# The first group's second product as seven products in seven PSUM banks, and the second group's attention between the units of its first product

## Chip, cores and metric

One core of a Trainium2 chip runs the kernel. The metric is the device time of one execution, in microseconds; lower is better.

## What is computed

The first part is a lightning attention over `q`, `k`, `v` of shape (4, 8, 768, 64) in float32: in blocks of positions, scores are masked by powers of a decay `lam`, and a state `k^T v` is carried from block to block. The second part takes its result as a matrix `x` of 3072 tokens by 512 and runs two products with an activation between them:

```python
x = attn_out.transpose(0, 2, 1, 3).reshape(3072, 512)
h = x @ w_in                  # 512 x 2048
g = h - np.tanh(h)
out = g @ w_out               # 2048 x 512, float32
```

The two weight matrices arrive as 64-bit floats. The kernel makes 32-bit floats of them itself.

## The kernel before

**Tiling.** The tokens are worked in six groups (`NG`), group g holding block g of 128 positions of all four batches, so 512 tokens. The 2048 hidden columns are four units (`NU`) of 512. Each group has attention for two pairs of batches (`attention(g)`: transposes, scores, output, state), the first product `x @ w_in` unit by unit, the activation, and the second product with `w_out`.

**Seven products in place of eight.** Groups 1 to 5 do both matrix products by the Winograd scheme: each factor is cut in four, sums of the parts are formed, and seven products of half size take the place of eight (`FACT` lists which sums meet in which product). Some of those products are cut once more (`down_twice`, `inner_steps`). Group 0 does neither, because its weights are still arriving: `up_plain(u, (c,))` makes one quarter c of unit u (11, 21, 12 or 22) by eight calls of a 128x128 by 128x256 matmul, then a tanh on ScalarE (L760) and a subtraction on VectorE (L761) put it into `hidden(0, c)`. `down_plain(kt)` (L766) then makes the second product row block by row block: for each of eight row blocks `kt` it issues eight matmuls 128x128 by 128x512 (L774), two for each of four batches, into four PSUM banks that stay open over all eight row blocks. Float32 matmuls are two instructions each in the trace, a pair of weight load and matmul for each of two passes.

**How weights arrive.** `load_weights` starts the DMA of a 128x512 block of 64-bit weights into one of four `raw64` buffers: blocks 0 to 15 are `w_in` (four for each unit, on SP's queue), blocks 16 to 31 are `w_out` (two for each row block, on POOL's queue). `weights(n)` makes the blocks up to n ready by `round_block`: three operations on ScalarE (L269 to L271) and two on VectorE (L273, L274), through one of two scratch tiles `r0`, `r1`. A block's buffer is free again after its last ScalarE operation. Calls of `weights` stand by hand between the units and the row blocks, and so set how far the loads run ahead.

**Row blocks and their stores.** A row block `kt` of `w_out` lies in one of two buffers `wt` (pool `wst`), which has room for four parts and four sums. `sums_out(kt)` (L244) forms the sums on VectorE (L247 to L250) and stores seven factors to DRAM on POOL's queue: two DMAs into `factors` (L252, L253) and one or two into `fine` (L256). The later groups read them from there. The next row block to use a buffer waits until its matmuls, sums and stores have ended. `sums_in(u)` (L237) forms in place, on VectorE, the sums of `w_in` that the groups from 1 on need.

**Order.** After group 0's attention the body runs `up_plain` for units 0 to 3 (L817 to L825), then the eight row blocks (L829 to L837). The pieces of group 1's attention stand behind row blocks 0 to 5 (`more`, L828), and `sums_in` behind the last four. Then the pools `stage`, `qpool` and `wst` close, `load_quarters` fetches factors back, and the loop over groups 1 to 5 begins with `up(1, 0, 1)` (L847). A scheduler may move instructions of one engine a little against this order where `keep_in_program_order` (or `tied`) doesn't forbid it; each engine executes its own list strictly in order.

Of the kernel before, what the change touches and what calls it, by code (L numbers as in the profile page):

```python
# [9 lines left out]
F32 = mybir.dt.float32  # L10
# [5 lines left out]
AF = mybir.ActivationFunctionType  # L16
AL = mybir.AluOpType

BLK = 128
# [5 lines left out]
def kernel(  # L25
# [32 lines left out]
    nc = tc.nc  # L58
    B, H, S, D = q.shape
    NTOK, DM = out.shape  # L60
    DFF = moe_w_in.shape[1]
    NP = H // 2
    KI = DM // 128
# [3 lines left out]
    NU = DFF // 512  # L67
    KH = KO // 2
# [35 lines left out]
    def powers():  # L104
        for j in range(2):
            tc.keep_in_program_order(nc.vector.tensor_copy(
                fwd[ts(j, 64), :, 0], lam_all.rearrange("s (p j) -> s j p", j=2)[ts(j, 64), j, :]))
        m = 1
        while m < BLK:
            tc.keep_in_program_order(nc.vector.tensor_tensor(  # L110
                fwd[:, :, m:2 * m], fwd[:, :, 0:m], fwd[:, :, m - 1:m].to_broadcast([128, NP, m]), op=AL.mult))
            m *= 2
# [68 lines left out]
    NX = 7  # L181
    factors = dram.tile([NX, 128, KH, 256], F32, name="factors")

    SUB = (1, 2, 6, 5, 7, 3, 4)
# [37 lines left out]
    def weights(n):  # L222

        while ready["done"] < min(n, len(blocks)):
            at_ = ready["done"]
            load_weights(at_ + WAHEAD)
            kind, n_, m = blocks[at_]
            if kind == "out" and m == 0:
                pair[n_] = wst.tile([128, 8, 256], F32, name="wt", tag="w")
            w = w1[n_][:, m] if kind == "in" else pair[n_][:, 2 * m:2 * m + 2]  # L230
            if at_ in wraw:
                round_block(w, wraw.pop(at_), at_ < 2 * KI)
            else:
                load_block(nc.gpsimd, w, kind, n_, m)
            ready["done"] += 1

    def sums_in(u):  # L237
        a11, a12, a21, a22 = (w1[u][:, 2 * c:2 * c + 2, r] for r, c in ((0, 0), (0, 1), (1, 0), (1, 1)))
# [3 lines left out]
            tc.keep_in_program_order(nc.vector.tensor_tensor(dst, x, y, op=op))  # L242

    def sums_out(kt):  # L244
        wt = pair[kt]
        b11, b12, b21, b22, t1, t2, t4, t3 = (wt[:, x] for x in range(8))
        nc.vector.tensor_tensor(t1, b12, b11, op=AL.subtract)  # L247
        nc.vector.tensor_tensor(t2, b22, t1, op=AL.subtract)
        nc.vector.tensor_tensor(t3, b22, b12, op=AL.subtract)
        nc.vector.tensor_tensor(t4, b21, t2, op=AL.subtract)  # L250
        f = factors[:].rearrange("x p k c -> p x k c")
        nc.gpsimd.dma_start(out=f[:, 0:1, kt, :], in_=wt[:, 0:1, :])  # L252
        nc.gpsimd.dma_start(out=f[:, 1:NX, kt, :], in_=wt[:, 2:8, :])  # L253

        for x, j in ((1, 0),) if kt % 2 == 0 else ((2, 0), (3, 1)):
            nc.gpsimd.dma_start(out=fine[:, SUB.index(x), :, kt // 2, :].rearrange("n p c -> p n c"),  # L256
                                in_=wt[:, 3:8, ts(j, 128)])

    def round_block(w, raw64, first):

# [15 lines left out]
    def bank(name, tag, bufs):  # L276
        return psum.tile([128, 512], F32, name=name, tag=tag, bufs=bufs)
# [143 lines left out]
    def hidden(g, c):  # L421

        if (g, c) not in hid:
            hid[g, c] = gpool.tile([128, NU, 2, HB], F32, name=f"g{c}", tag=f"g{c}")
        return hid[g, c]
# [198 lines left out]
    def otile(name):  # L624
        return opool.tile([128, 512], F32, name=name, tag="o")
# [99 lines left out]
    def every(steps):  # L725
        for _ in steps:
            pass
# [15 lines left out]
    def up_plain(u, cs):  # L743

        hm = {}
        for c in cs:
            a, t = divmod(c - 11, 10)
            hm[c] = bank("h", ("ya", "yb", "z", "w")[2 * t + a], 1).rearrange("q (m c) -> q m c", m=2)
        for i in range(KI):
            for c in cs:  # L750
                a, t = divmod(c - 11, 10)
                for m in range(2):
                    tied(u == 0, nc.tensor.matmul(  # L753
                        out=hm[c][:, m, :], lhsT=w1[u][:, i, a, ts(m, 128)], rhs=xt[0, t][:, i, :],
                        start=m == 0 and i == 0, stop=i == KI - 1, skip_group_check=True))
                if (i, c) != (KI - 1, cs[-1]):
                    yield
        for c in cs:
            th = work.tile([128, 2, HB], F32, name="th", tag="th")
            nc.scalar.activation(th, hm[c], AF.Tanh)  # L760
            nc.vector.tensor_tensor(hidden(0, c)[:, u], hm[c], th, op=AL.subtract)  # L761
        yield

    obank = {}

    def down_plain(kt):  # L766
        wt = pair[kt]
        for b in range(B):
            if kt == 0:
                obank[b] = bank("op0", ("ya", "yb", "z", "w")[b], 1)  # L770
            i, t = divmod(b, 2)
            for a in range(2):
                g = hidden(0, 11 + i + 10 * a)[:, kt // 2, kt % 2, ts(t, 128)]
                nc.tensor.matmul(out=obank[b], lhsT=g, rhs=wt[:, 2 * a:2 * a + 2, :], start=kt == 0 and a == 0,  # L774
                                 stop=kt == KH - 1 and a == 1)
            if kt == KH - 1:
                ob = opool.tile([128, DM], F32, name="ob", tag="o")
                nc.scalar.activation(ob, obank[b], AF.Copy)
                nc.gpsimd.dma_start(out=out[b * S:b * S + BLK, :], in_=ob)


    def run(pieces):
        for fn, *args in pieces:
            fn(*args)
# [30 lines left out]
    every(half)  # L815
    weights(2 * KI)
    every(up_plain(0, (12, 22)))  # L817
    for u in range(1, NU):
        for c in (11, 21, 12, 22):
            every(up_plain(u, (c,)))  # L820
            weights(ready["done"] + 1)
        if u == 2:
            load(2 * B)
        if u == 1:
            powers()  # L825
    p0, p1 = attention(1)
    weights(len(blocks) - 2 * (KH - 2))
    more = [p0[0:1], p0[1:2], p0[2:], p1[0:1], p1[1:2], p1[2:]]  # L828
    for kt in range(KH):  # L829
        down_plain(kt)  # L830
        sums_out(kt)
        if kt + 2 < KH:
            weights(ready["done"] + 2)
        if kt < len(more):
            run(more[kt])
        if kt >= KH - NU:
            sums_in(kt - KH + NU)  # L837
    early.close()
    late["blk"] = ctx.enter_context(tc.tile_pool(name="blk", bufs=2 * B - 1))
    late["pool"] = ctx.enter_context(tc.tile_pool(name="late", bufs=1))  # L840
# [7 lines left out]
    for g in range(1, NG):  # L848
        last = g == NG - 1
        p0, p1 = attention(g + 1) if not last else ([], [])  # L850
        for u in range(NU):
            for n in (2, 6, 5, 7, 1, 4, 3) if g < GI else (1, 7, 3) if u == 0 else (6, 5, 1, 7, 3) if u + 1 < NU else (
                    6, 5, 7, 1, 3):
                if n != 1:
                    up(g, u, n)
                elif u + 1 < NU:
                    up(g, u + 1, 1)
                else:
                    every(down(g, 1))
                if g in turns:  # L860
                    made.append(n)
                    step = len(made) - turns[g][0]
                    for t, first in turns[g][1]:
                        if step == first:
                            if t > 1:
                                load_quarters(t)
                            making[t] = factors_twice(t)
                        if first <= step < first + 4:
                            next(making[t])
            if g == GI - 1:  # L870
                inner_weights(u)
            if not last and u > 1:
                run(p0[u - 2:u - 1])
        if twice(g, 4):
            sums_twice(g, 4)
        every(down(g, 2))
        run(p0[2:])
        sums_twice(g, 5)
        every(down_twice(g, 4, "z") if twice(g, 4) else down(g, 4))
        run(p1[0:1])  # L880
        sums_once(g, 21, 21, 11)
        sums_twice(g, 6)
        every(down_twice(g, 5, "w"))
        run(p1[1:2])
        if twice(g, 7):
            sums_twice(g, 7)
        every(down_twice(g, 6, "z"))
        if twice(g, 3):
            sums_twice(g, 3)
        run(p1[2:])  # L890
        every(down_twice(g, 7, "w") if twice(g, 7) else down(g, 7))
        if last:
            down_end(g)
            continue
        inner_tokens(g + 1)
        p3 = down_twice(g, 3, "z") if twice(g, 3) else down(g, 3)
        p2 = inner_steps(g + 1, 2, "yb")
        for kind, _ in in_turn(g):
            next(p3 if kind == "down" else p2)
        every(p2)  # L900
        every(p3)
        p4 = inner_steps(g + 1, 4, "yb")
        for n in (None, None, 1, None, None, 6, None, None, 5, None):
            if n is None:
                next(p4)
            else:
                up(g + 1, 0, n)
        every(p4)
# [30 lines left out]
```

## Time and profile before

| | us |
|---|---|
| median of 3 runs | 675.35 (675.31 to 678.8) |
| the profiled execution: its own time | 675.67 |
| its span in the profile | 673.8 |
| TensorE (PE) busy in the span | 661.6 |
| VectorE (DVE) busy | 451.1 |
| ScalarE (ACT) busy | 214.8 |
| GpSimd (POOL) busy | 199.5 |

The page gives, for each engine, busy time and its share of the span, then slices, DMA queues, the chain of work that ended last, and groups of instructions by line. 1.87 us of the profiled execution's time lie outside its span. A line number with L is one of the kernel before, unless it is said to be the changed kernel's.

### The profile page before, as it was taken

To read this page: it belongs to the slowest core of one execution; us is meant where nothing else is said; L and a number is where in the kernel's file an instruction comes from. 1 tells how busy PE (TensorE), PEld (TensorE's weight loads), DVE (VectorE), ACT (ScalarE), POOL (GpSimd) and SP (SyncE) were. 2 spreads that over 40 slices of the span, in tenths; PEclk is the share of its full clock that TensorE was granted. 3 is DMA by queue.
4 is the path that set the end of the run, shared out by engine and by line. 5 is a ranking of instruction groups with operands and counts; after the bars stand their busy time and mean duration, and the time that the engine had idled before them with its cause. 6 is when DMAs were issued, how large, how long until landed. Compare 5 with 4: busy or idle time off the path is not lost.

```text
span 673.8 us, 12802 instructions
## 1 busy us (share of the span) xinstructions
PE 661.6 (98%) x4824; PEld 576.0 (85%) x4824; DVE 451.1 (67%) x808; ACT 214.8 (32%) x405; POOL 199.5 (30%) x345
## 2 busy tenths in 40 slices
PE   8899999999999999999999999999999999999997
PEld 6688855458888999988999988899988899988997
DVE  4476454792887772499896378888358977357743
ACT  4797454523321111333112243112333122234110
POOL 0002333235332334144345201254300245400351
PEclk9999999999999999999999999999999999999999
DMA  9979769788655978587798742698830677610494
GB/s 210 220 223 288 258 202 286 231 242 244 178 142 129 242 200 212 123 249 230 219 287 254 186 79 51 157 280 245 245 75 8 164 235 217 217 38 1 126 293 160
DMA packets 162716, 128.79 MB, mean 191 GB/s; under 512 B 133856, under 2 KB 135008, under 8 KB 162656
## 3 DMA queue, kind: packets, MB, share of 16 engines
q0 software_dynamic: 28976, 96.49, 45.2%
q1 hardware_dynamic: 133536, 31.50, 23.7%
q8 instruction: 38, 0.62, 0.4%
q14 instruction: 22, 0.18, 0.1%
q10 hardware_dynamic: 144, 0.00, 0.0%
HBM read 103.55 MB, written 24.38 MB: 190 GB/s over the span
## 4 chain that ended last, share of the span: by engine, by line
PE 92%; DMA 2%; SPq 2%; issue 1%; POOL 1%; ACT 0%; DVE 0%; POOLq 0%; ACTq 0%
PE y L436 16%; PE z L436 10%; PE y L698 10%; PE op L774 8%; PE h L753 7%; PE zw L698 7%; PE w L645 5%; PE y L645 5%; PE y L520 4%; PE plain L645 3%; PE sp L330 3%; PE op L384 3%; PE z L520 2%; PE op L378 2%; PE kv L352 1%
## 5 line engine op out<-in xcount | busy, mean ns | idle before, releaser
L610 POOL DMA_DIRECT2D wb<-fine x147 | 79.2, 539 | 115.0 <-PE y L698 48.3
L444 ACT ACTIVATE th<-g 128x512 f32<-128x512 f32 x76 | 47.6, 630 | 99.0 <-DVE g L449 33.2
L613 POOL DMA_DIRECT2D wb<-factors x56 | 30.2, 541 | 155.6 <-PE y L645 97.3
L436 PE MATMUL y<-xt,w 128*128 128x256 f32 x320 | 74.0, 380 | 0.0
L436 PEld LDWEIGHTS y<-xt,w 128*128 128x128 f32 x320 | 59.9, 190 | 9.0 <-ACT g L524 0.9
L701 ACT ACTIVATE q<-y 128x128 f32<-128x128 f32 x84 | 23.3, 278 | 129.2 <-PE y L698 124.4
L445 DVE TENSOR_TENSOR g<-g,th 128x512 f32<-128x512 f32 x76 | 52.0, 690 | 18.2 <-ACT th L444 18.1
L753 PE MATMUL h<-xt,w 128*128 128x256 f32 x256 | 56.5, 381 | 1.3 <-DVE w L274 1.3
L774 PE MATMUL op<-wt,g 128*128 128x512 f32 x128 | 56.5, 595 | 0.0
L753 PEld LDWEIGHTS h<-xt,w 128*128 128x128 f32 x256 | 48.2, 190 | 8.5 <-DVE w L274 1.0
L698 PE MATMUL y<-wb,g 128*128 128x128 f32 x384 | 51.1, 278 | 0.0
L774 PEld LDWEIGHTS op<-wt,g 128*128 128x128 f32 x128 | 23.8, 190 | 27.7 <-issue 26.5
L698 PEld LDWEIGHTS y<-wb,g 128*128 128x128 f32 x384 | 46.4, 192 | 1.2 <-issue 0.3
L436 PE MATMUL z<-tt,ws 128*128 128x256 f32 x160 | 38.0, 380 | 0.0
L436 PE MATMUL z<-xt,ws 128*128 128x256 f32 x160 | 37.9, 380 | 0.0
L436 PE MATMUL y<-tt,ws 128*128 128x256 f32 x160 | 37.8, 379 | 0.0
L645 PE MATMUL y<-wb,g 128*128 128x256 f32 x160 | 35.6, 379 | 0.5 <-PE y L436 0.5
L645 PE MATMUL w<-wb,g 128*128 128x256 f32 x160 | 35.8, 382 | 0.0
L334 DVE TENSOR_TENSOR ss<-sp,mask 128x512 f32<-128x512 f32 x48 | 31.1, 685 | 6.3 <-PE sp L330 6.3
L645 PEld LDWEIGHTS y<-wb,g 128*128 128x128 f32 x160 | 30.3, 190 | 5.0 <-PE y L436 0.9
L205 POOL DMA_DIRECT2D raw<-in_moe_w_out_dram x16 | 9.3, 583 | 83.8 <-DMA raw<-in_moe_w_in_dram 52.0
L436 PEld LDWEIGHTS z<-xt,ws 128*128 128x128 f32 x160 | 30.3, 190 | 4.3 <-ACT g L452 0.2
(168 smaller groups left out, 1293.2 us busy)
## 6 DMA issues: line engine op xcount, KB each, us to landing
wb<-fine POOLq DMA_DIRECT2D x147, 256.0 KB, 4.1
wb<-factors POOLq DMA_DIRECT2D x68, 256.0 KB, 4.2
raw<-in_moe_w_out_dram POOLq DMA_DIRECT2D x16, 512.0 KB, 6.6
v_nat<-in_v_dram SPq DMA_DIRECT2D x24, 256.0 KB, 5.4
factors<-wt POOLq DMA_DIRECT2D x8, 768.0 KB, 5.5
wb<-fine_in POOLq DMA_DIRECT2D x24, 256.0 KB, 4.3
k_nat<-in_k_dram SPq DMA_DIRECT2D x20, 256.0 KB, 5.0
raw<-in_moe_w_in_dram SPq DMA_DIRECT2D x8, 512.0 KB, 6.0
```

Of the source, the lines that this page charges most:

```text
L334: tied(g == 0, nc.vector.tensor_tensor(ss[:, j], sp[j], mask[:, j], op=AL.mult))
L436: nc.tensor.matmul(out=t[:, m, :], lhsT=wt[:, kt, ts(m, 128)], rhs=x[:, kt, :], start=first and m == 0 and kt == 0, stop=kt == 1, skip_gro ...
L444: nc.scalar.activation(th, src, AF.Tanh)
L445: nc.vector.tensor_tensor(dst(c), src, th, op=AL.subtract)
L520: nc.tensor.matmul(out=dst[:, ts(u, 128)], lhsT=a, rhs=b, start=x in (1, 2, 5) and u == 0, stop=True, skip_group_check=True)
L610: nc.gpsimd.dma_start(out=t.rearrange("p m c -> p (m c)"), in_=fine[TWICE.index(n_), SUB.index(x_)].rearrange("p u c -> p (u c)"))
L613: nc.gpsimd.dma_start(out=t, in_=factors[XAT[FACT[n_][1]]][:, 2 * x_:2 * x_ + 2, :])
L645: nc.tensor.matmul(out=t[:, m, :], lhsT=a[:, u, kt, ts(m, 128)], rhs=wb[:, kt, :], start=first and u == 0 and m == 0 and kt == 0, stop=u = ...
L698: nc.tensor.matmul(out=dst, lhsT=a[:, u, :], rhs=wb[:, ts(u, 128)], start=x in (1, 2) and u == 0, stop=u == NU - 1, skip_group_check=True)
L701: nc.scalar.activation(keep, dst, AF.Copy)
L753: tied(u == 0, nc.tensor.matmul(out=hm[c][:, m, :], lhsT=w1[u][:, i, a, ts(m, 128)], rhs=xt[0, t][:, i, :], start=m == 0 and i == 0, stop= ...
L774: nc.tensor.matmul(out=obank[b], lhsT=g, rhs=wt[:, 2 * a:2 * a + 2, :], start=kt == 0 and a == 0, stop=kt == KH - 1 and a == 1)
```

## The change

The second product of group 0 becomes seven products as well. `down_first(kt, ns)` adds row block kt to the products listed in ns; each product has an accumulator of its own: four in the single banks (`ya`, `w`, `z`, `yb`) and three in banks of the attention's pool (`att`, four banks). The sums on the hidden side are formed in place: `sums_first(u)` after each unit, and `sums_late(kt)` within each row block, after its products 1 and 2. `first_results` adds the seven accumulators up and stores four results. The row blocks get a third buffer: every third one lies in `ws[3]` (parts) and `ws[2]` (sums), which `sums_in(2)` and `sums_in(3)` need only later; these two move into group 1. The stores of one row block become five or seven DMAs where they were three or four. Group 1's attention moves from between the row blocks to between the units 2 and 3, whose quarters take turns, and its loads for the first two batches move ahead.

```diff
--- before.py
+++ after.py
@@ -226,13 +226,20 @@
             load_weights(at_ + WAHEAD)
             kind, n_, m = blocks[at_]
             if kind == "out" and m == 0:
-                pair[n_] = wst.tile([128, 8, 256], F32, name="wt", tag="w")
-            w = w1[n_][:, m] if kind == "in" else pair[n_][:, 2 * m:2 * m + 2]
+                pair[n_] = pair_tiles(n_)
+            w = w1[n_][:, m] if kind == "in" else pair[n_][0][:, 2 * m:2 * m + 2]
             if at_ in wraw:
                 round_block(w, wraw.pop(at_), at_ < 2 * KI)
             else:
                 load_block(nc.gpsimd, w, kind, n_, m)
             ready["done"] += 1
+
+    def pair_tiles(kt):
+
+        if kt % 3 == 2:
+            return tuple(ws[u].rearrange("p x k c -> p (x k) c")[:, 0:4] for u in (3, 2))
+        wt = wst.tile([128, 8, 256], F32, name="wt", tag="w")
+        return wt[:, 0:4], wt[:, 4:8]
 
     def sums_in(u):
         a11, a12, a21, a22 = (w1[u][:, 2 * c:2 * c + 2, r] for r, c in ((0, 0), (0, 1), (1, 0), (1, 1)))
@@ -242,19 +249,22 @@
             tc.keep_in_program_order(nc.vector.tensor_tensor(dst, x, y, op=op))
 
     def sums_out(kt):
-        wt = pair[kt]
-        b11, b12, b21, b22, t1, t2, t4, t3 = (wt[:, x] for x in range(8))
+        bt, tt = pair[kt]
+        b11, b12, b21, b22 = (bt[:, x] for x in range(4))
+        t1, t2, t4, t3 = (tt[:, x] for x in range(4))
         nc.vector.tensor_tensor(t1, b12, b11, op=AL.subtract)
         nc.vector.tensor_tensor(t2, b22, t1, op=AL.subtract)
         nc.vector.tensor_tensor(t3, b22, b12, op=AL.subtract)
         nc.vector.tensor_tensor(t4, b21, t2, op=AL.subtract)
         f = factors[:].rearrange("x p k c -> p x k c")
-        nc.gpsimd.dma_start(out=f[:, 0:1, kt, :], in_=wt[:, 0:1, :])
-        nc.gpsimd.dma_start(out=f[:, 1:NX, kt, :], in_=wt[:, 2:8, :])
+        nc.gpsimd.dma_start(out=f[:, 0:1, kt, :], in_=bt[:, 0:1, :])
+        nc.gpsimd.dma_start(out=f[:, 1:3, kt, :], in_=bt[:, 2:4, :])
+        nc.gpsimd.dma_start(out=f[:, 3:NX, kt, :], in_=tt[:, 0:4, :])
 
         for x, j in ((1, 0),) if kt % 2 == 0 else ((2, 0), (3, 1)):
-            nc.gpsimd.dma_start(out=fine[:, SUB.index(x), :, kt // 2, :].rearrange("n p c -> p n c"),
-                                in_=wt[:, 3:8, ts(j, 128)])
+            dst = fine[:, SUB.index(x), :, kt // 2, :].rearrange("n p c -> p n c")
+            nc.gpsimd.dma_start(out=dst[:, 0:1], in_=bt[:, 3:4, ts(j, 128)])
+            nc.gpsimd.dma_start(out=dst[:, 1:5], in_=tt[:, 0:4, ts(j, 128)])
 
     def round_block(w, raw64, first):
 
@@ -761,22 +771,48 @@
             nc.vector.tensor_tensor(hidden(0, c)[:, u], hm[c], th, op=AL.subtract)
         yield
 
-    obank = {}
-
-    def down_plain(kt):
-        wt = pair[kt]
-        for b in range(B):
+    acc = {}
+    ACC = {1: ("ya", 1), 2: ("w", 1), 5: ("z", 1), 6: ("yb", 1), 7: ("att", 4), 4: ("att", 4), 3: ("att", 4)}
+    FIRST = {1: (11, 0, 0), 2: (21, 0, 2), 3: (21, 0, 3), 4: (22, 1, 2), 5: ("S1", 1, 0), 6: (11, 1, 1), 7: (12, 1, 3)}
+
+    def sums_first(u):
+        g11, g12, g22, s1 = (hidden(0, c)[:, u] for c in (11, 12, 22, "S1"))
+        nc.vector.tensor_tensor(s1, g12, g22, op=AL.add)
+        nc.vector.tensor_tensor(g12, g11, g12, op=AL.subtract)
+
+    def down_first(kt, ns):
+
+        u, m = divmod(kt, 2)
+        for n in ns:
             if kt == 0:
-                obank[b] = bank("op0", ("ya", "yb", "z", "w")[b], 1)
-            i, t = divmod(b, 2)
-            for a in range(2):
-                g = hidden(0, 11 + i + 10 * a)[:, kt // 2, kt % 2, ts(t, 128)]
-                nc.tensor.matmul(out=obank[b], lhsT=g, rhs=wt[:, 2 * a:2 * a + 2, :], start=kt == 0 and a == 0,
-                                 stop=kt == KH - 1 and a == 1)
-            if kt == KH - 1:
-                ob = opool.tile([128, DM], F32, name="ob", tag="o")
-                nc.scalar.activation(ob, obank[b], AF.Copy)
-                nc.gpsimd.dma_start(out=out[b * S:b * S + BLK, :], in_=ob)
+                acc[n] = bank("acc", *ACC[n]).rearrange("q (m c) -> q m c", m=2)
+            c, part, x = FIRST[n]
+            a, b = hidden(0, c)[:, u, m], pair[kt][part][:, x]
+            for r in range(2):
+                nc.tensor.matmul(out=acc[n][:, r, :], lhsT=a[:, ts(r, 128)], rhs=b, start=kt == 0 and r == 0,
+                                 stop=kt == KH - 1, skip_group_check=True)
+
+    def sums_late(kt):
+        u, m = divmod(kt, 2)
+        g11, g21, s1 = (hidden(0, c)[:, u, m] for c in (11, 21, "S1"))
+        nc.vector.tensor_tensor(g11, s1, g11, op=AL.subtract)
+        nc.vector.tensor_tensor(g21, g21, g11, op=AL.subtract)
+
+    def first_results():
+        flat = {n: t.rearrange("q m c -> q (m c)") for n, t in acc.items()}
+        q, o11, q5, o12 = (otile(x) for x in ("q1", "o11", "q5", "o12"))
+        nc.scalar.activation(q, flat[1], AF.Copy)
+        nc.vector.tensor_tensor(o11, q, flat[2], op=AL.add)
+        store(0, 11, o11)
+        nc.vector.tensor_tensor(q, q, flat[6], op=AL.add)
+        nc.vector.tensor_tensor(q5, q, flat[5], op=AL.add)
+        nc.vector.tensor_tensor(q, q, flat[7], op=AL.add)
+        nc.vector.tensor_tensor(o12, q5, flat[3], op=AL.add)
+        store(0, 12, o12)
+        nc.vector.tensor_tensor(q, q, flat[4], op=AL.add)
+        store(0, 21, q)
+        nc.vector.tensor_tensor(q5, q5, flat[7], op=AL.add)
+        store(0, 22, q5)
 
 
     def run(pieces):
@@ -815,26 +851,39 @@
     every(half)
     weights(2 * KI)
     every(up_plain(0, (12, 22)))
-    for u in range(1, NU):
-        for c in (11, 21, 12, 22):
-            every(up_plain(u, (c,)))
-            weights(ready["done"] + 1)
-        if u == 2:
-            load(2 * B)
-        if u == 1:
-            powers()
+    sums_first(0)
     p0, p1 = attention(1)
-    weights(len(blocks) - 2 * (KH - 2))
-    more = [p0[0:1], p0[1:2], p0[2:], p1[0:1], p1[1:2], p1[2:]]
+    load(B + 2)
+    turns = [(1, 11, 1, ()), (1, 21, 1, ()), (1, 12, 1, ()), (1, 22, 1, ()), (2, 11, 2, p0[0:1]), (2, 21, 2, p0[1:2]),
+             (3, 11, 1, ()), (3, 21, 1, p0[2:4]), (2, 12, 1, ()), (2, 22, 1, p1[0:1]), (3, 12, 1, p1[1:2]),
+             (3, 22, 1, ())]
+    for u, c, n, more in turns:
+        every(up_plain(u, (c,)))
+        weights(ready["done"] + n)
+        run(more)
+        if c == 22:
+            sums_first(u)
+            if u == 1:
+                load_weights(NU * KI)
+                load(2 * B)
+                powers()
+            if u == 2:
+                sums_in(0)
+    sums_out(0)
+    run(p1[2:4])
+    weights(NU * KI + 6)
+    run(p1[4:])
     for kt in range(KH):
-        down_plain(kt)
-        sums_out(kt)
-        if kt + 2 < KH:
+        down_first(kt, (1, 2))
+        if kt + 1 < KH:
+            sums_out(kt + 1)
+        sums_late(kt)
+        down_first(kt, (5, 4, 7, 6, 3) if kt + 1 < KH else (5, 6, 7, 4, 3))
+        if kt + 3 < KH:
             weights(ready["done"] + 2)
-        if kt < len(more):
-            run(more[kt])
-        if kt >= KH - NU:
-            sums_in(kt - KH + NU)
+        if kt == 2:
+            sums_in(1)
+    first_results()
     early.close()
     late["blk"] = ctx.enter_context(tc.tile_pool(name="blk", bufs=2 * B - 1))
     late["pool"] = ctx.enter_context(tc.tile_pool(name="late", bufs=1))
@@ -857,6 +906,8 @@
                     up(g, u + 1, 1)
                 else:
                     every(down(g, 1))
+                if g == 1 and u < 2 and n == 5:
+                    sums_in(u + 2)
                 if g in turns:
                     made.append(n)
                     step = len(made) - turns[g][0]
```

## Prediction

> **What bounds the kernel now.** I read the page's busy times first, then the waits of PE, then the stretch of the change in the table by stage, then the chain of waits.
>
> ```profile
> PE 661.6 (98%) x4824; PEld 576.0 (85%) x4824; DVE 451.1 (67%) x808; ACT 214.8 (32%) x405; POOL 199.5 (30%) x345
> ```
>
> PE is busy for 661.6 of 673.8 us. That is an average, so the stages matter. The stage table (columns: PE, PEld, DVE, ACT, POOL busy, granted clock, DMA share, GB/s):
>
> ```profile
> 31.14:81.48 50.34, 50.34 (x233) 44.35 (x234) 30.79 (x64) 39.53 (x68) 9.82 (x15) 1.00 0.94 268
> 81.48:154.00 72.52, 71.11 (x418) 38.35 (x417) 45.03 (x89) 29.53 (x48) 22.70 (x32) 1.00 0.77 229
> 154.00:202.00 48.00, 48.00 (x224) 42.24 (x224) 32.36 (x67) 15.74 (x26) 19.77 (x31) 1.00 0.70 190
> ```
>
> The first stretch is units 0 to 3 of the first product, the second the row blocks with group 1's attention between them, the third the start of group 1. In all three PE is full. ACT is at 39.5 of 50.3 us in the first: keep that in mind. PE's waits between 31 and 154 us are two:
>
> ```profile
> PE tp L314 <- DVE wt L273: 1.4, 1, 1.4
> PE h L753 <- DVE w L274: 0.6, 1, 0.6
> ```
>
> After 150 us PE's list of waits adds up to 1.4 us. So what PE saves before 154 us arrives at the end, unless it turns into a new wait. The chain of waits prices the pieces (start, us, what, instructions):
>
> ```profile
> 31.14 50.34 PE h L753 x232
> 81.48 6.87 PE op L774 x16
> 88.35 1.75 PE tp L314 x16
> 90.09 6.87 PE op L774 x16
> 96.96 1.99 PE sp L330 x32
> 98.95 7.06 PE op L774 x16
> 106.01 1.03 PE op L378 x32
> 107.05 1.90 PE op L384 x32
> 108.95 0.93 PE kv L352 x32
> ```
>
> **What is removed and added on PE.** The eight row blocks at L774 take 6.87+6.87+7.06+7.08+6.87+7.06+13.93 = 55.74 us. The seven products are 7 x 8 row blocks x 2 = 112 calls with 256 columns, the form of L753: 232 instructions, 116 calls, in 50.34 us is 0.434 us a call. 112 x 0.434 = 48.6 us: **7.1 us less**. A half-width call could cost more than half; but L774 gives 6.87/8 = 0.859 us a call for 512 columns, so 256 cost half, and the weight load (190 ns) stays under the 217 ns of its matmul.
> The attention keeps its work, 1.75+1.99+1.03+1.90+0.93 = 7.60 us for each pair, 15.2 us. Between 116.95 and 120.28 its second transposes took 3.33 us, 1.58 over 1.75: VectorE's decay of `k` stood behind a rounding (L273) that waited for the buffer of a row block, and a transpose for that. With the attention ahead of the row blocks this place is gone: **1.6 us less**. Together 8.7; with no new wait the row blocks end at 154.0-8.7 = 145.3 in place of 154.0, and the time is 675.67-8.7 = 667.0.
>
> **New waits, by the built order.** I took each engine's list of the changed kernel in its built order, with what each waits for, and laid the rows' durations along it. From start to start: ACT's three operations of a block 0.57+0.63+0.63 = 1.83; its tanh and copies about 0.48; DVE 0.60 for 512 columns and for L274, 0.34 for 256 and for L273. Up to unit 1's end at 53.7 (31.14 + 52 calls) PE's list is unchanged.
>
> First place, block 15. ACT's list now has all four tanhs of unit 1 ahead of block 11; before, blocks 11 to 13 stood between them. The last tanh ends at 54.3, so blocks 11 to 15 come after it: 11 to 56.1, 12 to 57.9, 13 to 60.5 (a tanh within), four copies of `qt`, `kt` to 62.5, a tanh to 63.0, block 14 to 64.85, the first operation of block 16, block 15 to 67.3; DVE adds 0.7: 68.0. PE, with transposes and scores between, wants block 15 at 67.0. **Wait: 1.0 us**. Nothing may be lost if its scores run late anyway; 3 if the DMA is late, because 1.5 MB of q, k, v now stand ahead of block 11 on SP: at 268 GB/s 5.9 us, against ACT's idle time of about that length before 54.3.
>
> Second place, bank z. `(3, 12)` needs it from `(2, 12)`, whose tanh stands on ACT behind the roundings of `w_out` blocks 16 to 23. These go in a chain: a load starts when a buffer is free and lands in 6.6 us (median of its row). By this row the tanh is at 84.2 and DVE done at 84.9, PE arrives at 84.9. I take 0.3 us, with 0 and 1.5 as ends. The row blocks so begin near 98.0.
>
> Third place, row block 3. A row block is 14 x 0.434 = 6.08 us. Its product 6 needs `sums_late` after 5 x 0.434 x 2 = 4.34 us. In row block 3 DVE's list has the second rounding of row block 5 ahead of `sums_late(3)`. That one waits for ACT, which starts block 26 only when PE leaves row block 2 (buffer `ws[3]`) and has four more operations on blocks 27 and 28 before it: 0.57 + 6 x 0.63 = 4.35, + 0.67 for the last, + 0.34 DVE, + 0.42 for the sum = 5.85. Product 6 waits 1.5 us. Then a rounding and one operation of `sums_in(1)` stand ahead of the second late sum: product 3 waits 0.7. **2.2 us**. Behind them on DVE wait only the sums of row block 5, needed six us later. The ends: 0 if the late sums are ready by other slack, 5 if block 28 lands 3 us late. In the other row blocks the roundings that stand ahead end by 2.7 us after the start, in time.
>
> **What I cost at nothing.** The 20 more DMAs on POOL: at 0.55 us of issue (L252) at most 11 us, where POOL is at 22.70 of 72.52; if that cover goes, row block stores slip (rival 3). The in-place sums (`sums_first`, `sums_late`): 8 x 0.60 + 16 x 0.34 = 10.2 us of DVE, which is at 45.03 of 72.52. `first_results`: seven DVE operations, 4.2 us; group 1's first products take other banks or the ones read first. `sums_in(2)`, `(3)` in group 1: 2.4 us each; before, DVE waits 7.3 us there for the first w bank, and product 5's z has 3.45 us of PE work between; without that cover up to 2.4. ws[2] and ws[3] hold stores that land well before. The loads of batches 6 and 7: k of batch 7 waits for the state matmul at 76.2, 5 to 7 us to land, wanted at 84.4: nothing, 0 to 1 us.
>
> [...] The row of 81.48 to 154 shows a granted clock of 1.00 in spite of a 1.41 us wait. [...]
>
> [...] Here `factors<-wt` lands in 6.7 us with 128 KB and 5.5 with 768 KB, so small ones are indeed not cheaper. [...]
>
> **Sum.** 8.7 - 1.0 - 0.3 - 2.2 = 5.2 us gained: 675.67 - 5.2 = 670.5 for a profiled execution. The median of the runs is 0.3 below the profiled one, so I say **670.2**.
>
> **Rivals.** About 0.5%, 3.4 us, is what a measurement of this kernel can tell from no change: the edges are 672.0 and 678.7.
> 1. *Forecast*, 668.2 to 672.0: two or three short waits of 2 to 5.3 us in all. Chance 0.50.
> 2. *No new wait worth naming*: 666.5 to 668.2. For it: PE waits two times in 123 us before, and the built order may hold slack that I don't see. Against it: the wait in row block 3 follows from lists in strict order. 0.22.
> 3. *The stores of a row block don't keep up*. A row block moves 2 x 512 KB in, 128 + 768 KB to `factors` and on average 480 KB to `fine`: 2.46 MB. At the stretch's best (388 GB/s, one of 40 slices) that is 6.3 us, more than 6.08; at the 268 GB/s of the first stretch 9.2 us. Row blocks 3 to 7 reuse buffers. For it: the stretch from 31 to 154 moves 30.2 MB, 245 GB/s, and must move nearly that in 118 us. Against it: three buffers, so a store has two row blocks' time (12 us) to land, and the stores of blocks 0 to 2 go out during the attention. If it binds in part, by about 1.4 us on each of five (7.5 us at 329 GB/s, the best 10 us slice), the time is 667.0 + 7.1 = 674.1 and up to 678.7 with the forecast's waits: within 0.5%. 0.20.
> 4. *Slower*: the same loop at 268 GB/s, 3.1 us on each of five row blocks, 15.7 us: 682.7. It decides from 12.0 us of waits on, 2.4 us a row block; place: the first rounding of row blocks 3 to 7, behind which `sums_late` stands on DVE. 0.08.
> That the change doesn't do what it says (112 calls not cheaper than 64) is excluded by the two rows of calls above.
>
> **Numbers.** Faster by over 0.5%: 0.50 + 0.22 = 0.72; within: 0.20; slower: 0.08. The range from 666.5 to 675.0 leaves out rival 4 and the upper part of rival 3, under 0.2.
>
> **What would show it.** PE's L774 rows gone, 224 instructions of 256 columns with about 217 ns each; attention(1) among L753's rows; PE's waits between 31 and the end of the row blocks naming DVE L274 of unit 3, and the late sums in row block 3, 2 to 5 us; the first product of group 1 starting near 148.8. If PE waits in every row block from 3 on, for DVE behind a store, it is rival 3 or 4. A wait in group 1 for DVE would show that `sums_in(2)` and `(3)` cost there.

## The result, and the profile after

The changed kernel takes **669.71 us** in the median (668.99 to 670.71); the kernel before, run beside it, 675.31. The ratio is 0.9913, with a 95% interval from 0.9884 to 0.9943. The profiled execution took 669.39 us with a span of 667.6: 6.28 us less than the profiled execution of before (675.67). Line numbers are now those of the changed kernel: its rounding is L279 to L284, a call of the first product L763 (before: L753), of the seven products L792, the late sums L798 and L799.

The page's busy times:

```profile
PE 655.6 (98%) x4920; PEld 594.1 (89%) x4920; DVE 466.4 (70%) x839; ACT 213.7 (32%) x402; POOL 210.8 (32%) x365
```

PE is still 98% busy, with 6.0 us less work: this was a change of PE's work, and PE's share hasn't moved. DVE has 15.3 us more. The table by stage (columns as before: PE, PEld, DVE, ACT, POOL, TensorE's granted clock as a share of full speed, DMA share, GB/s):

```profile
31.08:98.60 67.52, 66.58 (x521) 58.02 (x521) 53.84 (x105) 50.49 (x87) 16.80 (x27) 1.00 0.95 265
98.60:147.15 48.55, 48.55 (x226) 42.76 (x226) 30.53 (x70) 17.75 (x27) 24.95 (x38) 1.00 0.81 250
147.15:195.00 47.85, 47.85 (x223) 42.12 (x223) 38.68 (x78) 15.15 (x25) 21.43 (x33) 1.00 0.71 195
```

The first row is now the units with group 1's attention among them: 0.94 us of PE are missing there. The second is the eight row blocks, full from end to end, and the third group 1, full too. PE's only wait from 31.6 to 160 us (engine, line, what it waited for, us, times, longest):

```profile
PE h L763 <- DVE w L284: 0.9, 1, 0.9
```

The chain of waits shows where it comes from, and prices the pieces (start, us, what):

```profile
59.63 0.60 ACT th L770
...
67.61 0.70 DVE w L284
...
68.35 4.58 PE h L763 x20
...
76.80 7.10 PE h L763 x32
83.90 1.75 PE tp L324 x16
...
98.60 48.54 PE acc L792 x224
147.15 1.73 PE y L446 x8
```

From 59.6 to 67.6 the chain runs through ScalarE: tanhs, copies of `qt` and `kt`, blocks 14 and 15. Then come DVE's last operation on block 15 and PE. Before that ScalarE had waited for PE's products, and it took up block 11 right behind unit 1's last tanh (the bracket is the idle time before the group and its releaser):

```profile
53.83 0.60 ACT L770 ACTIVATE th<-h 128x512 f32<-128x512 f32 x1 [2.86 <-PE h L763]
54.32 0.67 ACT L279 ACTIVATE w<-raw 128x512 f32<-128x512 f32 x1
```

The transposes take 1.75 us; their wait of 1.58 us is gone. The row blocks end at 147.15 in place of 154.00: 6.85 us earlier. From there to the end of the span it is 520.45 us where it was 519.8: 0.65 us are given back later.

### The profile page after: what moved, and what is told of

Its sections match the earlier page's. It is cut to its first block, busy times and chain, and to the rows that moved or that the text cites. A ratio compares the mean times of both kernels' runs of the same rounds, so it can differ in the third digit from the quotient of the medians.

```text
span 667.6 us, 13061 instructions
## 1 busy us (share of the span) xinstructions
PE 655.6 (98%) x4920; PEld 594.1 (89%) x4920; DVE 466.4 (70%) x839; ACT 213.7 (32%) x402; POOL 210.8 (32%) x365
## 4 chain that ended last, share of the span: by engine, by line
PE 79%; issue 9%; DMA 5%; POOL 2%; SPq 2%; ACT 1%; DVE 1%; DVEq 0%; POOLq 0%; ACTq 0%
PE y L446 12%; PE y L708 10%; PE acc L792 7%; PE zw L708 7%; PE h L763 7%; PE z L446 7%; PE w L655 4%; PE y L655 4%; PE y L530 4%; PE plain L655 3%; PE sp L340 3%; PE op L394 3%; PE z L530 2%; DMA wb<-fine 2%; PE op L388 1%
## 5 line engine op out<-in xcount | busy, mean ns | idle before, releaser
L763 PE MATMUL h<-xt,w 128*128 128x256 f32 x256 | 58.0, 383 | 2.3 <-DVE w L284 2.3
L763 PEld LDWEIGHTS h<-xt,w 128*128 128x128 f32 x256 | 47.7, 190 | 10.2 <-DVE w L284 2.6
L344 DVE TENSOR_TENSOR ss<-sp,mask 128x512 f32<-128x512 f32 x48 | 31.1, 684 | 6.3 <-PE sp L340 6.3
L655 PEld LDWEIGHTS w<-wb,g 128*128 128x128 f32 x160 | 30.1, 190 | 4.4
L708 PE MATMUL zw<-wb,g 128*128 128x128 f32 x256 | 33.8, 275 | 0.0
```

What stands on the lines that cost most here:

```text
L344: tied(g == 0, nc.vector.tensor_tensor(ss[:, j], sp[j], mask[:, j], op=AL.mult))
L655: nc.tensor.matmul(out=t[:, m, :], lhsT=a[:, u, kt, ts(m, 128)], rhs=wb[:, kt, :], start=first and u == 0 and m == 0 and kt == 0, stop=u = ...
L708: nc.tensor.matmul(out=dst, lhsT=a[:, u, :], rhs=wb[:, ts(u, 128)], start=x in (1, 2) and u == 0, stop=u == NU - 1, skip_group_check=True)
L763: tied(u == 0, nc.tensor.matmul(out=hm[c][:, m, :], lhsT=w1[u][:, i, a, ts(m, 128)], rhs=xt[0, t][:, i, :], start=m == 0 and i == 0, stop= ...
```

## Experiments

All ratios are to the kernel before on the same chip.

**The move alone.** The kernel before, with its eight plain products and two buffers, but the attention where the change puts it:

```diff
+    turns = [(1, 11, 1, ()), ... , (2, 11, 2, p0[0:1]), (2, 21, 2, p0[1:2]), (3, 11, 1, ()), (3, 21, 1, p0[2:4]), ...]
+    for u, c, n, more in turns:
+        every(up_plain(u, (c,)))
+        weights(min(ready["done"] + n, NU * KI + 4))
+        run(more)
```

> The kernel before with one part of the change alone: attention(1) and the load of batches 6 and 7 go between the units of the first product; the row blocks stay eight plain products of 512 columns with two buffers. Theory (the seven products carry the gain, the move is worth its removed wait less the wait that it makes at block 15): -1.6 for the second transposes' wait, +1.2 for block 15, about +0.4 for the pieces that follow scores and outputs: 674 to 676, no change, and PE's row blocks 55 us without a wait. Rival (the move is the main gain): 671 or less. A second rival (with two buffers the roundings bind as soon as nothing stands between the row blocks): PE waits inside the row blocks, 678 or more.

Measured: 675.18 us, ratio 1.0003 (0.999 to 1.0017). Its wait on DVE and its row blocks, from the list of PE's waits and the chain:

```profile
PE h L753 <- DVE w L274: 1.2, 1, 1.2
```

```profile
98.55 55.13 PE op L774 x128
```

The theory holds: the move gives 1.6 us and takes them again. It also corrects a term. Eight plain products in a row are 55.13 us, not the 55.74 they took between attention pieces, so the seven products by themselves save 55.13 - 48.54 = 6.59 us. The other 0.6 us are what PE loses when it comes back from small matmuls to wide ones (before, the row blocks behind scores and outputs took 7.06 to 7.08 us where the others took 6.87), and the move only carries that along: behind the outputs and scores the pieces L763 take 4.58, 7.10 and 3.65 us where 10, 16 and 8 calls at 0.434 are 4.34, 6.94 and 3.47, together 0.58 more.

**The attention in one lump behind the units.**

```diff
-    turns = [(1, 11, 1, ()), ... ]
+    turns = [(u, c, n, ()) for u, ns in ((1, (1, 1, 1, 1)), (2, (2, 2, 1, 1)), (3, (1, 1, 1, 1)))
+             for c, n in zip((11, 21, 12, 22), ns)]
...
-    run(p1[2:4])
+    run(p0)
+    run(p1[0:4])
```

> The kernel after with attention(1) in one lump after the units, which run in the order 1, 2, 3; the seven products and their three buffers stay. Theory (the seven products carry the gain; block 15's wait comes from the attention's loads and copies between the units' weights): the wait at block 15 is gone, -1.2, and inside the lump the transposes, scores and decays wait for each other for 1 to 4 us: 669 to 673. Rival (putting it between the units is needed for the gain): 675 or more, with the waits inside the lump at 5 us or more.

Measured: 677.6 us, ratio 1.004 (1.0024 to 1.0057): the rival. PE's three longest waits from 31.6 to 160 us (a fourth is 0.5), then two stretches behind one another:

```profile
PE tp L324 <- DMA q_nat<-in_q_dram: 2.2, 1, 2.2
PE op L388 <- DVE ss L344: 1.9, 2, 1.7
PE sp L340 <- ACT kt L326: 1.0, 1, 1.0
```

```profile
85.56:88.97 3.41, 1.51 (x22) 1.07 (x24) 3.41 (x7) 0.00 (x0) 2.72 (x6) 1.00 1.10 380
88.97:92.40 3.43, 3.43 (x46) 3.10 (x48) 3.15 (x6) 0.00 (x0) 0.53 (x1) 0.51 1.06 328
```

Block 15's wait is gone as expected, but PE waits inside the lump, 5.6 us in all: 2.9 for steps of the attention on the other engines, and 2.7 for q and k of the second pair, whose transfers come late (k's starts at 93.97 in the chain, behind the first pair's state matmul). And there is a second price that I hadn't in the sum: behind the waits of 1.0 and 1.7 us the granted clock is 0.51 for 3.43 us (second row), which costs about 1.7 us more (an estimate, 3.43 x 0.49). 5.6 - 0.9 + 1.7 = 6.4 of the 7.1 us by which group 1 starts later (154.27 against 147.15); the rest, 0.7, I can't place. So the seven products are the gain, and the place between the units is what keeps it.

**The loads later.**

```diff
-    load(B + 2)
     turns = [(1, 11, 1, ()), ... ]
...
+        if (u, c) == (1, 12):
+            load(B + 2)
```

> The kernel after with the load of batches 6 and 7 moved behind the third product of unit 1, so that three w_in blocks go ahead of q, k, v on the SP queue and between unit 1's tanhs on ScalarE. Theory (block 15 waits since blocks 11 to 15 all come after unit 1's tanhs on ScalarE): the 0.9 us wait for block 15 goes, 668.5, between 668.2 and 669.2. Rival (block 15 is late because its transfer is, or the wait is made up for later on PE): no change within 0.3 us, or the wait moves to the first transpose, which then stands behind q's load.

(The loads that move are those of batches 4 and 5, group 1's first pair; the expectation names the wrong ones.) Measured: 674.42 us, ratio 0.9974 (0.9958 to 0.9991), 3 to 5 us slower than the kernel after: both theories failed in size. Two stretches, then PE's timeline:

```profile
66.80:70.20 3.40, 1.13 (x4) 0.68 (x4) 3.18 (x6) 3.15 (x6) 0.53 (x1) 1.00 0.89 219
70.20:77.10 6.90, 5.96 (x14) 4.79 (x15) 5.73 (x12) 6.17 (x12) 2.12 (x4) 0.51 0.81 285
```

```profile
67.81 1.13 PE L763 MATMUL h<-xt,w 128*128 128x256 f32 x4 [1.01 <-DVE w L284]
71.14 7.54 PE L763 MATMUL h<-xt,w 128*128 128x256 f32 x20 [2.21 <-DVE w L284]
```

Blocks 14 and 15 now stand behind q, k and v on SP; in the chain the transfer of block 14 takes 9.60 us from 54.96, and ScalarE can start on it only at 64.6. PE waits 1.01 and 2.21 us, and then the clock is halved from 70.2 to 77.1: 20 instructions take 7.54 us where the kernel after has 4.58. 3.22 - 0.94 us of waits, 7.54 - 4.58 of clock and 0.44 by which the units started later (31.52 against 31.08) are 5.7 of the 6.1 us by which group 1 starts later. The mean granted clock of the executions points the same way: the one at 1.00 took 669.97 us, the three at 0.995 took 674.7 to 675.8. That ScalarE's order makes block 15 wait in the kernel after is shown by its own timeline above, not by this run, where the transfers came too late to tell; what the run shows is that the room to mend the wait is bounded from the other side by the transfers.

**Two buffers in place of three.**

```diff
-        if kt % 3 == 2:
-            return tuple(ws[u].rearrange("p x k c -> p (x k) c")[:, 0:4] for u in (3, 2))
...
-        if kt + 3 < KH:
+        if kt + 2 < KH:
             weights(ready["done"] + 2)
```

(The roundings ahead of the row blocks also stop two blocks earlier, at `NU * KI + 4`, since there is no third buffer to round into.)

> The kernel after with two buffers for the row blocks of w_out in place of three, the rest as it is. Theory (ScalarE's roundings and the stores have slack in the row blocks, so the third buffer is worth little): 0 to +3 us, as short waits of PE for the late sums, which stand behind roundings on VectorE. Rival (the stores of a row block take longer than the 6.07 us that PE needs, and the third buffer hides them): a wait in every row block from the third on, 1.2 us or more each, +7 to +15 us.

Measured: 673.25 us, ratio 0.9976 (0.9958 to 0.9993), 3.5 us slower than the kernel after by the medians. PE's longest wait in the row blocks (another is 0.5, for a late sum; lines are two lower in this kernel), and a piece of the chain:

```profile
PE acc L790 <- DVE wt L282: 1.1, 1, 1.1
```

```profile
135.95 5.90 DMA raw<-in_moe_w_out_dram
141.87 0.67 ACT wt L277
...
144.61 5.45 PE acc L790 x24
```

Nearer to the theory: single waits, not one in every row block. The 1.1 us come by a load, though: it is issued at 135.95, right behind five stores on POOL's queue of which the first waited for a sum, lands at 141.87, and ScalarE, DVE and PE follow. ScalarE's longest wait, 5.79 us before 126.70, is for a load that POOL issued at 119.5 to 120.6, behind stores again. The row blocks take 150.06 - 98.75 = 51.3 us in place of 48.5, so the third buffer is worth 2.8 us in the profiled executions and 3 to 4 by the times.

**Both halves of a row block held to its end.** Products 3 and 6 multiply other parts of the row block (so the output is another, the work the same):

```diff
-    FIRST = {..., 3: (21, 0, 3), ..., 6: (11, 1, 1), ...}
+    FIRST = {..., 3: (21, 0, 1), ..., 6: (11, 0, 2), ...}
```

> The kernel after with products 3 and 6 multiplying other parts of the row block (3 the half that product 1 reads, 6 the other half): the same amount of work in the same order, other values in the output. Both halves of a buffer are now held to the row block's last product, so that ScalarE can start no rounding of the third row block ahead before PE has left this one. This is the assumption with which the third place was predicted. Theory (the wait of row block 3 failed to come because product 1 alone reads the first half and frees it 5 us earlier): a wait for the late sums appears in row block 3 and perhaps in 4 and 6, 0.5 to 2.5 us together, 670.2 to 672.2. Rival (there was slack on ScalarE and VectorE anyway): no wait, no change within 0.3 us.

Measured: 670.52 us, ratio 0.9925 (0.9905 to 0.9946): no change beside the kernel after, and no wait over 0.2 us in the list of the row blocks. But the slack is used up: they take 148.96 - 100.04 = 48.92 us in place of 48.54. From DVE's timeline the late sum of row block 3, then pieces of the chain:

```profile
122.76 0.41 DVE L798 TENSOR_TENSOR g<-gS,g 128x256 f32<-128x256 f32 x1
```

```profile
100.04 17.48 PE acc L792 x80
...
117.54 0.68 ACT ws L279
...
123.22 25.74 PE acc L792 x118
```

In the kernel after the late sum ran at 119.01 in a row block that began near 116.8; here at 122.76 in one that began near 118.2. The chain now goes the way that the prediction feared, from PE's release of the buffer through ScalarE and the late sum back to PE, but PE loses 0.4 us and not 1.5. So the early release of the first half is part of the answer, not all: the rest of ScalarE's work on these two blocks (L280, L281) stands ahead of the release here, from 114.51 to 117.3, where the prediction had it behind.

**Six products.** The seventh is left out in all row blocks, and the results take the sixth's accumulator twice:

```diff
-        down_first(kt, (5, 4, 7, 6, 3) if kt + 1 < KH else (5, 6, 7, 4, 3))
+        down_first(kt, (5, 4, 6, 3) if kt + 1 < KH else (5, 6, 4, 3))
```

> The kernel after without the seventh product in the eight row blocks: its 16 calls are left out, and the results take another accumulator in its place. Theory (PE alone sets the pace of the row blocks, everything else has slack): 16 x 0.434 = 6.9 us less, 662.8, and 5.2 us a row block without waits. Rival (the stores or the roundings are close to binding at 6.07 us a row block): waits in the row blocks take back 2 us or more, 664.8 or above.

Measured: 664.79 us, ratio 0.9846 (0.9825 to 0.9867). The row blocks take 140.64 - 98.31 = 42.3 us in place of 48.5, with one wait of 0.4 us for a late sum: rounding, loads and stores keep up even at 5.2 us a row block, which speaks against rivals 3 and 4. But 1.2 us come back behind them (521.66 us to the end of the span against 520.45), with one wait of 1.5 us in group 1. From the timelines of DVE and PE there:

```profile
177.26 0.69 DVE L603 TENSOR_TENSOR wt<-oq,wt 128x512 f32<-128x512 f32 x1 [1.75 <-DMA fine<-wt]
```

```profile
178.61 1.99 PE L446 MATMUL z<-xt,ws 128*128 128x256 f32 x8 [1.54 <-DVE g L477]
```

DVE waits there for a store of its buffer `wt`, and the sum that PE needs (L477) is next in its list; in the kernel after DVE has no wait at this operation. The 0.65 us given back in the kernel after are not explained by this. PE's listed waits there are 1.7 us (1.0 for `wb<-fine`, 0.7 for a sum in group 2) against 1.4 in the kernel before. And the lump and the later loads, which reach group 1 at 154.27 and 153.22, so about when the kernel before does, need 520.73 and 520.28 us from there: it is not only that PE arrives earlier. The kernel after's two repeats below need 521.31 and 520.71, the move alone, with the old row blocks, 519.62. What the seven products add there stays open.

**Unit 3 later.** Can block 15's wait be had? One swap:

```diff
-             (3, 11, 1, ()), (3, 21, 1, p0[2:4]), (2, 12, 1, ()), (2, 22, 1, p1[0:1]), (3, 12, 1, p1[1:2]),
+             (2, 12, 1, ()), (3, 11, 1, p0[2:4]), (3, 21, 1, ()), (2, 22, 1, p1[0:1]), (3, 12, 1, p1[1:2]),
```

> The kernel after with one swap in the order of the products: the third product of unit 2 goes ahead of unit 3's first, so that PE wants unit 3's last two blocks 3.47 us later; every load and rounding keeps its place. Theory (the only wait of PE between 31 us and the end of the row blocks is for block 15 on VectorE, and nothing behind it has this wait as its cover): the 0.9 us go, 668.7, between 668.2 and 669.3. Rival (something behind it, the second pair's transposes or bank z, is late next): no change within 0.3 us of the kernel after, with a new wait behind 68 us.

> The swap of the run before together with the later load of e3_loads_later (what that load brings are q, k, v of the first pair, batches 4 and 5). There blocks 14 and 15 were late by 1.0 and 2.2 us, and the granted clock was 0.50 for the 6.9 us after it. Now PE wants these blocks 3.47 us later. Theory (the later load cost nothing but these two waits and the clock behind them): both waits under 0.3 us, clock 1.00, 668.7 to 669.7, so 4.5 us or more better than e3_loads_later. Rival (the later load costs by itself, in the copies of q and k or in what stands behind them on SP): 671 or more.

> The kernel after once more, on the chip of these two, as their reference: 669.7, and a granted clock of 1.00 in every execution, since its waits of 0.9 us are followed by full work.

On one chip: the kernel after 670.68 us, ratio 0.9928 (0.9913 to 0.9943); the swap 670.19, 0.9937 (0.9914 to 0.996); the swap with the later loads 671.5, 0.995 (0.9932 to 0.9969). The rival was right. Block 15's wait is gone with the swap, but (ScalarE, then PE):

```profile
83.31 0.78 ACT L280 ACTIVATE r<-raw 128x512 int16<-128x512 uint32 x1 [1.55 <-DMA raw<-in_moe_w_out_dram]
...
84.58 1.05 ACT L398 ACTIVATE xt<-op 128x512 f32<-128x512 f32 x2
```

```profile
85.19 0.66 PE L324 MATMUL tp<-ident,q_nat 128*128 128x128 f32 x4 [1.39 <-ACT xt L398]
```

ScalarE's list now has the roundings of four `w_out` blocks ahead of the copies that empty the attention's banks, one of them waits for its transfer, and the second pair's transposes find no bank. With the later loads this wait is 2.3 us, block 15's is gone and the clock of the profiled execution stays at 1.00. Group 1 starts 4.3 us earlier there than with the later loads alone (148.93 against 153.22), near the 4.5 I gave; by the medians it is 2.9 us, by the ratios 1.6, with intervals that overlap. The time itself is the rival's. The repeated kernel after had block 15's wait at 1.4 us; there ScalarE first stood idle for 1.05 us until block 11's transfer had landed (55.06 in place of 54.32), so the wait is not the order's alone. Its expectation on the clock fails: single executions of it show 0.997. In the profiled one that lies in the start (0.93 in the mean over the first 25 us, of which PE is busy for 21.06).

**The copies ahead.** The swap again, with ScalarE's copies held ahead of four roundings, or of one:

```diff
-            tied(g == 0, nc.scalar.activation(xt[g, half][...], ops[x], AF.Copy))
+            tied(g <= 1, nc.scalar.activation(xt[g, half][...], ops[x], AF.Copy))
...
-                round_block(w, wraw.pop(at_), at_ < 2 * KI)
+                round_block(w, wraw.pop(at_), at_ < 2 * KI or NU * KI + 2 <= at_ < NU * KI + 6)
```

(With one, the last condition is `at_ == NU * KI + 5`.)

> The swap of e7_unit3_later, and on ScalarE the copies of the first pair's outputs ahead of the roundings of w_out blocks 19 to 22, which waited for their transfers there and let PE's second transposes wait 1.4 us. Theory (the two waits are the only loss between 31 us and the row blocks' end, and the roundings of these four blocks have until 110 us): no wait over 0.3 us up to the row blocks, which start near 97.5; 1.0 to 1.6 us less than the kernel after, 668.1 to 668.9 beside 669.7. Rival (ScalarE has no slack between 60 and 110 us, something is always late): a wait of about 1 us again, in row block 2 or at the scores, and no gain beyond 0.3 us.

> The kernel after once more, on the chip of the run before, as its reference: 669.7 to 670.7, with block 15's wait of 0.9 to 1.4 us.

> As e10_copies_ahead, but only one w_out block (the second of row block 2) is held behind the copies of the first pair's outputs, in place of four. Theory (in e10 the four late roundings pushed the sums and the roundings of the third and later row blocks on VectorE ahead of the late sums of row blocks 0 and 3; with one block they keep their place): no wait over 0.5 us between 31 us and the row blocks' end, 1.0 us or more less than the kernel after by the ratios to the kernel before, a ratio of 0.990 or less. Rival (every order of this list leaves some wait of 1 to 2 us, since ScalarE and VectorE are full from 60 to 90 us): a wait of 1 us or more in another place and a ratio of 0.991 to 0.994.

With four: 671.97 us, ratio 0.9938 (0.9918 to 0.9958); the kernel after beside it 669.92, 0.9914 (0.9894 to 0.9934). Both waits of the swap are gone and the row blocks start at 97.06, as expected, and then PE waits in them. With four, ScalarE, DVE and PE in row block 3:

```profile
119.74 0.78 ACT L280 ACTIVATE r<-raw 128x512 int16<-128x512 uint32 x1 [2.22 <-DMA raw<-in_moe_w_out_dram]
...
121.01 0.63 ACT L279 ACTIVATE ws<-raw 128x512 f32<-128x512 f32 x1
```

```profile
121.67 0.43 DVE L283 TENSOR_SCALAR ws<-ws 128x512 uint32<-128x512 uint32 x1 [4.52 <-ACT ws L279]
122.02 0.42 DVE L798 TENSOR_TENSOR g<-gS,g 128x256 f32<-128x256 f32 x1
```

```profile
122.49 1.13 PE L792 MATMUL acc<-wt,g 128*128 128x256 f32 x4 [1.07 <-DVE g L798]
```

This is the third place of the prediction, operation by operation: the second rounding of row block 5 stands ahead of the late sums on DVE, waits for ScalarE, and ScalarE for block 28's transfer. It costs 1.07 us here and 0.41 at the second late sum; a late sum in row block 0 costs 1.38. With one block held, 670.08 us, ratio 0.9933 (0.9911 to 0.9955), PE's waits from 31.6 to 160 us:

```profile
PE tp L324 <- DVE state L368: 0.7, 1, 0.7
PE acc L792 <- DVE g L799: 0.4, 1, 0.4
PE acc L792 <- DVE g L798: 0.3, 1, 0.3
```

The rival again: 1.4 us in three other places. None of these orders beats the kernel after. From 55 to 90 us it has DVE busy for 32.9 and ACT for 31.1 of 35 us, so there is little room left: in each order tried, what one operation gained another lost.

## Why the prediction was right, and where not

- **Seven products, -7.1:** measured 55.74 - 48.54 = 7.2. A half-width call costs half, as worked out: 48.54/112 = 0.433 us, where a full-width one took 55.13/64 = 0.861 in the move alone. But the term mixed two things, as the move alone showed: 6.6 us of products and 0.6 us of coming back from small matmuls, which stay with the attention and are missing from the sum of 8.7.
- **Second transposes, -1.6:** right.
- **First place, block 15, 1.0:** PE waited from 67.4 to 68.35, 0.94 us; predicted was 67.0 to 68.0. The order of ScalarE's list, with durations from rows of before, gave place, cause and size in this execution. Over the kernel after's three profiles it was 0.9 to 1.4; in the two repeats (1.2 and 1.4) ScalarE had also waited 0.78 and 1.05 us for block 11's transfer. That is the late DMA for which the prediction kept its upper end.
- **Second place, bank z, 0.3:** no wait, its lower end.
- **Third place, row block 3, 2.2:** the step that failed. "Starts block 26 only when PE leaves row block 2" is true of block 27, whose half of the buffer product 3 reads, but only product 1 reads block 26's half. In the kernel after the timelines show ScalarE at it 4.7 us before PE leaves row block 2, and the late sums in time:

```profile
112.07 0.67 ACT L279 ACTIVATE ws<-raw 128x512 f32<-128x512 f32 x1
...
118.00 0.64 ACT L279 ACTIVATE ws<-raw 128x512 f32<-128x512 f32 x1
```

```profile
119.01 0.42 DVE L798 TENSOR_TENSOR g<-gS,g 128x256 f32<-128x256 f32 x1
```

  I had taken a whole buffer where the release goes by what each product reads. That is not all: with both halves held to the end PE lost 0.4 us, since the operations that I had counted behind the release mostly ran ahead of it. (The sum is 5.78 us by its own terms, not 5.85; nothing hangs on it.) The place itself is real: with four blocks held later the wait came, 1.5 us, and in the swap and the later loads, where the chain goes through block 28's transfer, the row blocks take 48.87 and 48.86 us, 0.3 more than in the kernel after.
- **Costed at nothing:** the stores and the DMAs on POOL keep up (six products: at 5.2 us a row block PE's one listed wait in them is 0.4 us, for a late sum). `sums_in(2)` and `(3)` cost nothing: the stage to 195 us is full. What I had not priced are the 0.65 us given back behind the row blocks; their cause stays open.
- **Clock:** the kernel after's wait of 0.94 us left the clock at 1.00, but in two other runs waits of 1 to 2.2 us were followed by a clock of 0.51, for 6.9 us (the later loads) and 3.43 us (the lump): see below. The sum priced each wait at its own length alone. In those two runs that would have been too little, by 7.54 - 4.58 = 2.96 us and by about 1.7 us.
- **Sum:** 8.7 - 3.5 = 5.2 predicted, 6.28 measured in the profiled execution. The difference is 2.5 of waits that didn't come, less 0.6 of restarts and 0.65 given back later; 0.2 stay open. So it was in part luck that the median of 669.71 came so near to 670.2: in place of two or three waits of 2 to 5.3 us in all came one of 0.94, nearer to what rival 2 says, and two losses that weren't in the sum, 1.25 us together, made up for half of the 2.5.

## What to carry to other kernels

Where PE is full on both sides of a change, count its calls: that gain arrived here, less 0.65 us that came back behind it. For a new wait, lay each engine's list out with measured durations, and release a buffer by the part that each instruction reads, not as a whole. When three engines are nearly full, expect a reorder to move a wait (each of the four tried here did); and look at the clock behind two short waits close together: in two of the runs here it was 0.51 there, for 6.9 and 3.43 us.

## What the runs showed of the hardware

Behind the first 25 us the clock fell in two of the profiled executions, without any wait over 2.21 us. In the later loads, waits of 1.01 and 2.21 us within 4.4 us were followed by a clock of 0.51 for 6.9 us (PE was busy for 1.13 of the 3.40 us ahead of the drop), and in the lump, waits of 1.0, 1.7 and 0.2 us by a clock of 0.51 for 3.43 us (busy 1.51 of 3.41). Single waits of 2.3 us (the swap with later loads), 1.4 (the swap) and 0.9 (the kernel after) left it at 1.00. So the longest gap alone didn't decide here: 2.3 us did nothing where 2.21 with a shorter one beside it did. Nor is every pair of waits followed by a drop: 2.18 and 0.48 us, later in the lump (95.4 to 100.4), left the clock at 1.00.

The share of work ahead doesn't order these runs either: a stretch of 3.4 us that holds the whole 2.3 us wait has 1.1 us of work in it, less than ahead of either drop, and the clock stayed at 1.00. What sets off a drop, and what sets its length, no run here shows. So a single wait of 2.3 us isn't shown to be safe.

The 256 KB halves of `w_in` blocks landed in 5.8 us in the median of the kernel after between 35 and 90 us, and in 8.1 with the later loads. There the last four are issued right behind q, k and v on SP's queue, where in the kernel after blocks 11 to 13 stand between them. ScalarE stood idle for 4.3 us until block 14 had landed.
